# A transformer block with full attention on one core: row-maxima tables cleared on VectorE, difference tile kept longer, all loaded blocks as candidates, unit-end tasks later

## The chip, the cores and the metric

The kernel runs on one core of a Trainium2 chip. The metric is the device time of one execution in microseconds (us); three runs of the kernel before took 1124.92, 1126.49 and 1126.60 us, median 1126.49 us. Lower is better.

## What is computed

```
mod = silu(c) @ w_mod                                 # six rows of 448: sa, ca, ga, sb, cb, gb
h = layernorm(x) * (1 + ca) + sa                      # x: 2048 tokens x 448
q, k, v = h @ wqkv                                    # 16 heads of 28
p = softmax(q @ k^T * 28**-0.5)                       # 2048 x 2048 per head, no mask
x = x + ga * ((p @ v) @ wo)
h = layernorm(x) * (1 + cb) + sb
x = x + gb * (gelu(layernorm(h) @ w1 + b1) @ w2 + b2) # 448 -> 1792 -> 448
```

## The kernel before, in words

**Phase 1** normalises x, transposes it and makes q, k and v. Each matrix is kept as a high part in a short float format and a low part with the rest, so a product takes three matmul terms. q and k of the four groups of heads (g = 0 to 3, four heads each, one per 32 rows of the TensorE array) go to DRAM by blocks of 512 tokens.

**Phase 2** is the attention: 256 steps. A unit u is a group g = u // 4 and a query block qt = u % 4 of 512 queries; a step is one of the 16 key tiles (kt) of 128 keys of a unit. A step issues on TensorE twelve score matmuls (L1287): three terms for the two heads of one half of the array's rows (rows 0 to 63), and three for the other half (rows 64 to 127). ScalarE takes the exponential of each half (L1300), and TensorE multiplies by v one step later (L1245). This needs the maximum of each row of scores ahead of the unit. It is put into the score product itself, as an extra row of the q tile; so for the *next* units the scores are also computed the other way round, queries on the PSUM partitions (L474, "maximum matmuls": 128 queries by 512 keys, one head), and VectorE reduces each (L479) into a table `mxp` of the pair (g, qt). There are 1024 such matmuls. In phase 2 they stand between the score matmuls. Up to step 118 there are four in an even step and three in an odd one, on three PSUM banks (`m1`, `m2`, `m2`). From step 119 (`RING`) VectorE reduces two at a time out of a 1024-wide tile (L674), about three in a step. TensorE runs a maximum matmul of one half of the rows beside score matmuls of the other half, so `emit_single(half, ...)` looks for a head of the half that is asked for.

The order of the maximum matmuls comes from a queue `mxq`. `ready_max` keeps of its *first 64 entries* those whose q and k blocks are loaded, and `emit_single` and `emit_pair` choose from these. `count` notes what is done: when a k block has served all its maxima, the block of the next group is loaded in its place (`load_hi`, L506, one DMA on the SyncE queue); when a pair (g, qt) is complete, `max_fin` reduces its table, `put` (later) transposes the result and writes it into the q tile, and the next group's q block is loaded. A block may be used three steps after its load was issued.

Up to step 118 some blocks are done in pairs: `make_kd` forms the difference of two k blocks on GpSimd (L599); `open_pair` multiplies q with it and ScalarE takes the relu; one step later `close_pair` adds the first block's scores and takes the maximum (L638). A pair saves VectorE one reduction.

A unit's end is a chain of small tasks placed at fixed steps behind the unit's end: `t_den` (a DMA spreads the denominators), `t_rec` (VectorE reciprocal, then on SyncE a DMA to DRAM, `drec`, and a DMA that broadcasts it back to 128 rows, L998), `t_split` (GpSimd multiplies, L1003), `t_split2` (VectorE casts the high part, L1013, GpSimd makes the low part, L1014; then the DMAs out, where the unit is staged), and for the last units `t_wo`: the output projection, twelve matmuls in each of the steps kt = 8 to 11 (nine for unit 11). `load_q` loads the next unit's q tile (L760, two DMAs), and `put`'s four DMAs (L526) go into that same tile, so they wait for it.

**Phase 3** is the MLP. Its order depends on nothing that the change touches.

Every engine works through its own list in order. SyncE's list issues the DMAs, and one that waits keeps all later ones back.

Of the kernel before, what the change touches and what calls it, by code (L numbers as in the profile page):

```python
# [33 lines left out]
LAST_MAX = NKT - 4  # L34
RING = 119
PAIR_AT = (2, 2, 0, 2)
WO_MAX = 3
YTAGS = [f"{a}{i}" for a in ("kh", "qh") for i in range(4)]
EPS = 1e-5
# [4 lines left out]
def tile_adaln_block(ctx: ExitStack, tc: tile.TileContext, x, wqkv, wo, w1, b1, w2, b2, c, w_mod, out):  # L44
# [415 lines left out]
    mxp = {}  # L460
# [7 lines left out]
    def max_mm(g, qt, i, j, k, ps=None):  # L468
        if (g, qt) not in mxp:
            mxp[(g, qt)] = sbt("mxp", [128, 4, 4, 4], bufs=6)  # L470
            pool.memset(mxp[(g, qt)], -3.0e38)
        m = (ps or ps_mx)()
        js = slice(32 * j, 32 * j + DH)
        pe.matmul(m, qh_sb[(g, qt)][js, i * 128 : (i + 1) * 128], k[js, :], start=True, stop=True)  # L474
        return m
# [61 lines left out]
    phase1 = [True]  # L537
    queued = set()

    def queue_max(g, qt, cch):  # L540
        if (g, qt, cch) in queued:
            return
        queued.add((g, qt, cch))
        left.setdefault((g, qt), 64)
        if (g, qt) in paired and cch < 2:
            if cch == 1:
                pxq.extend((g, qt, i, j) for i in range(4) for j in range(4))
            return
        for i in range(4):
            for j in range(4):  # L550
                mxq.append((g, qt, cch, i, j))
        mxq.sort(key=lambda m: (m[:2] != (0, 0), -m[0] if phase1[0] else m[0], m[1:]))

    pair_no = {}

# [29 lines left out]
    def there(kind, g, b):  # L585
        return (g, b) in (qh_sb, kh_sb)[kind] and loaded.get((kind, g, b), 0) <= clock[0]

    def ready_max():
        return [m for m in mxq[:64] if there(1, m[0], m[2]) and there(0, *m[:2])][: 24 if clock[0] >= RING else 64]

    def by_set(m):
        return (m[:4], m[4] // 2)
# [1 line left out]
    kd = {"g": None, "from": 0}  # L594

    def make_kd(g):
        c0 = PAIR_AT[g]
        kd.update(g=g, t=slot("d0h", [128, 1, 512]), **{"from": clock[0] + 1})
        pool.tensor_tensor(out=kd["t"][:, 0, :], in0=f(kh_sb[(g, c0 + 1)]), in1=f(kh_sb[(g, c0)]), op=ALU.subtract)  # L599

    def other(m):
        return m[:2] + (m[2] + 1,) + m[3:]

    def pairable():
        return [
            m for m in mxq
            if m[2] == PAIR_AT[m[0]] and m[4] > 1 and other(m) in mxq and not (m[:2] == (0, 3) and m[3] > 1)
        ]

    def kept_back():  # L610
        kept = set()
        n = 0
        for m in pairable() if clock[0] < RING else ():
            n += 1
            if n <= (NKT * (m[0] * NB + m[1] - 1) + LAST_MAX - clock[0]) // 2 - 1:
                kept.update((m, other(m)))
        return kept
# [361 lines left out]
    def unit_end_tasks(u, o_sb):  # L979
# [57 lines left out]
            return go  # L1037


        times = (0, 4, 8, 9) if staged else (0, 1, 4, 5)  # L1040
        tasks = list(zip(times, (t_den, t_rec, t_split, t_split2)))
        if not staged:
            tasks += [(7 + t, t_wo(t)) for t in range(4)]
# [177 lines left out]
    def is_wo(s_):  # L1221
        return s_ // NKT >= NU - NB and 8 <= s_ % NKT < 12
# [30 lines left out]
    for u in range(NU):  # L1253
        g, qt = divmod(u, NB)
        for kt in range(NKT):
            step = u * NKT + kt
            if kt == 4 and u + 1 < NU and u + 1 not in qst:
                load_q(u + 1)
            clock[0] = step
            if kt == LAST_MAX and u + 1 < NU:  # L1260
# [3 lines left out]
                three = True  # L1264
                s_ring[:] = ["s0", turns[step % 2], turns[1 - step % 2]]
            now[0] = turns[step % 2]
            first = step % 2 if step >= RING else 0
            pt = {hf: slot(tags[step % len(tags)], [128, 2, 512], F32) for hf, tags in zip((first, 1 - first), ptags)}
            was, ring = ring, step >= RING and (three or not is_wo(step))
            if ring != was:  # L1270
                third_tile(ring)
            more = ring and not three and extra(step)
# [5 lines left out]
            ks, qs = kst[(g, kt // 4)], qst[u]  # L1278
            kc = slice((kt % 4) * 128, (kt % 4 + 1) * 128)
            for n, hf in enumerate((first, 1 - first)):  # L1280
                s2 = ps_s2() if three else ps_two((now[0] if n else "s0") if ring else ("s0", "s1")[n])
                for term, (kp, qp) in enumerate(((0, 0), (1, 0), (0, 1))):
                    if ring and n == 1 and term == 2 and mxq:
                        emit_pair(first, ps_two(turns[1 - step % 2]))
                    for jj in range(2):
                        rows_ = slice(64 * hf + 32 * jj, 64 * hf + 32 * jj + DH + (term == 0))
                        pe.matmul(s2[:, jj, :], ks[rows_, kp, kc], qs[rows_, qp, :], start=(term == 0), stop=(term == 2))  # L1287
                    if closing:
                        if (n, term) == (0, 0):
                            close_pair()  # L1290
                    elif n == 0 and term < n0 <= n_max:
                        emit_single(1, ps_mx)
                    if n == 1 and term == 2:
                        for _ in range(2 if closing else n_max - n0):
                            emit_single(0, ps_mx)
                    if ring and (n, term) == ((1, 0) if late_one else (0, 0)) and not three:
                        emit_single(1 - first, ps_mx)
                    if n == 1 and term == 2 and more:
                        emit_single(first, ps_mx)
                act.activation(pt[hf], s2, AF.Exp, scale=SCALE)  # L1300
# [131 lines left out]
```

## Time and profile before

| | |
|---|---|
| runs | 1124.92, 1126.49, 1126.60 us; median 1126.49 |
| the profiled execution's own time | 1128.93 us, span 1127.2 us |
| TensorE (PE) busy | 1113.3 us, 99% |
| VectorE (DVE) busy | 803.6 us, 71% |
| ScalarE (ACT) busy | 695.2 us, 62% |
| GpSimd (POOL) busy | 216.5 us, 19% |

One profiled execution is read. The page gives busy time by engine and groups of instructions; a group's last part is the idle time of the engine just before its instructions, with what ended it. The timeline gives single instructions as start, duration, engine, line, operation, tiles. PEld is TensorE's weight load, which overlaps the matmuls, and SPq is SyncE's queue. Step n's start is the start of its first score matmul (L1287). By these, phase 1 lasts up to 173 us, steps 0 to 118 to 480 us, steps 119 to 255 to about 831 us, the MLP to the end.

### The profile page before, as it was taken

Reading aid. Unit: us, or ns where it says so; the run is one execution under the profiler, and the core shown is the slowest. Engines: PE = TensorE matmul, PEld = TensorE weight load, DVE = VectorE, ACT = ScalarE, POOL = GpSimd, SP = SyncE. Lnnn points to the kernel's source line nnn. Section 1 sums busy time; section 2 is a strip of 40 time slices with the busy share of each in tenths; the row PEclk is TensorE's granted clock in tenths of the full one; section 3 lists DMA queues with packets and bytes.
Section 4 is the critical chain, followed back from the end, with each engine's and each line's share of the span. In section 5 each row is a group of like instructions: output and inputs, shape, how many; then the busy total and the mean of one; then the engine's idle time right before and its main releaser. Section 6 shows DMA issues by size and latency. Waiting matters only on the chain.

```text
span 1127.2 us, 20699 instructions
## 1 busy us (share of the span) xinstructions
PE 1113.3 (99%) x8319; PEld 675.3 (60%) x8319; DVE 803.6 (71%) x1380; ACT 695.2 (62%) x878; POOL 216.5 (19%) x228
## 2 busy tenths in 40 slices
PE   9999999999999999999999999999999999999998
PEld 6656765444445544444444444545468888888887
DVE  6869787979998889988888867584648853444322
ACT  4555757878888888888888867586852321111110
POOL 1543432110000000000100011205314504123000
PEclk9999999999999999999999999999999999999999
DMA  8553354131122111232210512121222100000000
GB/s 304 192 173 109 106 176 128 29 95 30 48 87 75 48 58 30 67 105 67 68 39 28 153 30 61 45 67 58 81 73 78 36 33 1 1 33 1 33 1 33
DMA packets 49342, 81.20 MB, mean 72 GB/s; under 512 B 12311, under 2 KB 18702, under 8 KB 49234
## 3 DMA queue, kind: packets, MB, share of 16 engines
q1 hardware_dynamic: 48762, 79.14, 22.5%
q8 instruction: 65, 1.06, 0.4%
q10 hardware_dynamic: 148, 0.46, 0.1%
q0 software_dynamic: 336, 0.28, 0.1%
q14 instruction: 31, 0.25, 0.1%
HBM read 55.04 MB, written 26.48 MB: 72 GB/s over the span
## 4 chain that ended last, share of the span: by engine, by line
PE 86%; DVE 2%; ACT 1%; DMA 1%; issue 1%; POOL 0%; SPq 0%; DVEq 0%; POOLq 0%; ACTq 0%
PE s L1287 21%; PE o L1245 21%; PE m L395 16%; PE m L474 7%; PE pa L395 5%; PE s L1367 3%; PE s L1368 3%; PE s L1366 3%; PE s L474 1%; PE t L1367 1%; PE t L1368 1%; PE t L1366 1%; DVE mxp L479 1%; DMA osb<-drec 1%; PE m L276 1%
## 5 line engine op out<-in xcount | busy, mean ns | idle before, releaser
L479 DVE TENSOR_REDUCE mxp<-m 128x1 f32<-128x512 f32 x564 | 364.2, 685 | 97.7 <-PE m L474 68.0
L1287 PE MATMUL s<-slot_b,slot_a 28*128 28x512 f32 (+1 forms) x3072 | 355.3, 424 | 1.7 <-DVE mxp L674 0.8
L1287 PEld LDWEIGHTS s<-slot_b,slot_a 28*128 28x128 f32 (+1 forms) x3072 | 211.1, 183 | 172.0 <-ACT slot_c L1300 93.3
L474 PE MATMUL m<-kh,qh 28*128 28x512 f32 x598 | 221.0, 462 | 2.3 <-DVE mxp L479 0.6
L1300 ACT ACTIVATE slot_c<-s 128x1024 f32<-128x1024 f32 x170 | 174.6, 1027 | 55.7 <-PE s L1287 52.4
L1245 PE MATMUL o<-slot_c,v 128*32 128x512 f32 x680 | 179.7, 607 | 0.0
L1343 ACT ACTIVATE full<-m,b_col 128x512 f32<-128x512 f32 x56 | 38.5, 688 | 191.9 <-PE m L395 179.7
L1245 PE MATMUL o<-slot_c1h,v 128*32 128x512 f32 x512 | 135.5, 608 | 0.9 <-ACT slot_c1h L1300 0.9
L1245 PE MATMUL o<-slot_c0h,v 128*32 128x512 f32 x512 | 134.7, 605 | 0.0
L1300 ACT ACTIVATE slot_c0h<-s 128x1024 f32<-128x1024 f32 x128 | 131.3, 1026 | 3.3 <-PE m L395 2.4
L674 DVE TENSOR_REDUCE mxp<-s 128x2 f32<-128x1024 f32 x105 | 128.6, 1225 | 4.2 <-PE s L474 0.2
L1300 ACT ACTIVATE slot_c1h<-s 128x1024 f32<-128x1024 f32 x128 | 130.7, 1021 | 0.0
L1346 DVE CAST hi<-full 128x512 fp32r<-128x512 f32 x56 | 25.2, 450 | 135.1 <-ACT full L1343 135.1
L1300 ACT ACTIVATE slot_d<-s 128x1024 f32<-128x1024 f32 x86 | 88.3, 1027 | 30.0 <-PE s L1287 28.4
L474 PEld LDWEIGHTS m<-kh,qh 28*128 28x128 f32 x598 | 92.4, 182 | 20.0 <-DVE mxp L479 12.0
L1003 POOL TENSOR_TENSOR osb<-osb,osb 128x512 f32<-128x512 f32 x16 | 21.1, 1318 | 398.0 <-DMA osb<-drec 332.1
L1245 PE MATMUL o<-slot_d,v 128*32 128x512 f32 x344 | 90.5, 605 | 0.4 <-ACT osb L1209 0.4
L395 PE MATMUL m<-y,slot_a 128*128 128x512 f32 x160 | 60.7, 395 | 0.0
L638 DVE CUSTOM_DVE_ANT_0 slot_d0i<-m,slot_d0i 128x512 f32<-128x512 f32 x55 | 38.0, 690 | 15.7 <-PE m L474 11.4
L1347 DVE TENSOR_TENSOR lo<-full,hi 128x512 fp32r<-128x512 f32 x56 | 44.1, 788 | 5.2
L1245 PEld LDWEIGHTS o<-slot_c,v 128*32 128x32 f32 x680 | 24.5, 108 | 38.1 <-issue 36.3
L474 PE MATMUL s<-kh,qh 28*128 28x512 f32 x210 | 46.5, 438 | 0.0
(340 smaller groups left out, 1847.4 us busy)
## 6 DMA issues: line engine op xcount, KB each, us to landing
slot_b<-d SPq DMA_DIRECT2D x32, 256.0 KB
slot_a<-d SPq DMA_DIRECT2D x32, 256.0 KB
d<-lo SPq DMA_DIRECT2D x28, 256.0 KB
d<-hi SPq DMA_DIRECT2D x16, 256.0 KB
osb<-drec SPq DMA_DIRECT2D x15, 256.0 KB
out_dram<-xn SPq DMA_DIRECT2D x16, 224.0 KB
raw<-in_B_w_dram SPq DMA_DIRECT2D x14, 224.0 KB
qh<-d SPq DMA_DIRECT2D x12, 256.0 KB
```

What stands on the lines that cost most here:

```text
L395: pe.matmul(p, a, b, start=(i == 0), stop=(i == len(terms) - 1))
L474: pe.matmul(m, qh_sb[(g, qt)][js, i * 128 : (i + 1) * 128], k[js, :], start=True, stop=True)
L479: dve.tensor_reduce(out=mxp[(g, qt)][:, i, j, cch : cch + 1], in_=m, op=ALU.max, axis=AX.X)
L674: dve.tensor_reduce(out=mxp[(g, qt)][:, i, j : j + 2, cch], in_=t, op=ALU.max, axis=AX.X)
L1245: pe.matmul(o[32 * j : 32 * j + 32, :], v_sb[kt // 4][:, kt % 4, 4 * g + j, :], p[j // 2][:, j % 2, :], start=(kt == 0), stop=(kt == NKT - 1),
L1287: pe.matmul(s2[:, jj, :], ks[rows_, kp, kc], qs[rows_, qp, :], start=(term == 0), stop=(term == 2))
L1300: act.activation(pt[hf], s2, AF.Exp, scale=SCALE)
L1343: act.activation(gf, p, AF.Gelu_apprx_tanh, bias=b1_col[:, i : i + 1])
L1347: dve.tensor_tensor(out=glo, in0=gf, in1=f(ghi), op=ALU.subtract)
L1366: pe.matmul(pp, ghi[:, ts], w_hi, start=(m == 0), stop=False)
L1367: pe.matmul(pp, ghi[:, ts], w_lo, start=False, stop=False)
L1368: pe.matmul(pp, glo[:, ts], w_hi, start=False, stop=(m == NFT - 1))
```

## The change

Nine edits, in the order of the file. (1) The tables of maxima: the table of (0, 0), all of whose entries are written anyway, is not cleared any more; those of the three pairs of phase 1 that skip an entry stay on GpSimd; the other twelve are cleared on VectorE. (2) `in_order` is the sort of `mxq` as a function; the order that it gives is the old one in phase 1, and in phase 2, where nothing of (0, 0) is left, too. (3) `ready_max` looks at all of `mxq`. (4) `make_kd` of the next group waits, two steps at a time, until no pairable block of the present one is left. (5) Which heads' rows are paired is read from `PAIR_ROWS`; the number of pairs in the program stays 55. (6) `kept_back` looks at no more pairs than there are steps for. (7) Unit-end tasks: for staged units the reciprocal and its two DMAs one step earlier, both splits one step later; for the others both splits one step later. (8) `load_q` at kt = 6 in place of 4. (9) Steps with projections take the halves in fixed order (`first` is 0 when `ring` is off), and before `RING` the two score tiles `s0` and `s1` change places.

```
-            pool.memset(mxp[(g, qt)], -3.0e38)
+            if (g, qt) != (0, 0):
+                (pool if (g, qt) in paired else dve).memset(mxp[(g, qt)], -3.0e38)
...
+    def in_order(m):
+        if phase1[0]:
+            return m[:2] != (0, 0), -m[0], m[1:]
+        return m[0], m[1], m[2:]
...
-        return [m for m in mxq[:64] if there(1, m[0], m[2]) and there(0, *m[:2])][: 24 if clock[0] >= RING else 64]
+        return [m for m in mxq if there(1, m[0], m[2]) and there(0, *m[:2])][: 24 if clock[0] >= RING else 64]
...
     def make_kd(g):
+        if g and any(m[0] == kd["g"] for m in pairable()):
+            at(clock[0] + 2, lambda: make_kd(g))
+            return
...
+PAIR_ROWS = {(0, 2): 2, (0, 3): 3, (1, 0): 2, (1, 1): 2}
-            if m[2] == PAIR_AT[m[0]] and m[4] > 1 and other(m) in mxq and not (m[:2] == (0, 3) and m[3] > 1)
+            if m[2] == PAIR_AT[m[0]] and m[4] > 1 and other(m) in mxq and m[3] < PAIR_ROWS.get(m[:2], 4)
...
-        for m in pairable() if clock[0] < RING else ():
+        for m in pairable()[: (RING - clock[0]) // 2] if clock[0] < RING else ():
...
-        times = (0, 4, 8, 9) if staged else (0, 1, 4, 5)
+        times = (0, 3, 9, 10) if staged else (0, 1, 5, 6)
...
-            if kt == 4 and u + 1 < NU and u + 1 not in qst:
+            if kt == 6 and u + 1 < NU and u + 1 not in qst:
                 load_q(u + 1)
...
-            first = step % 2 if step >= RING else 0
+            was, ring = ring, step >= RING and (three or not is_wo(step))
+            first = step % 2 if ring else 0
...
-                s2 = ps_s2() if three else ps_two((now[0] if n else "s0") if ring else ("s0", "s1")[n])
+                s2 = ps_s2() if three else ps_two((now[0] if n else "s0") if ring else ("s1", "s0")[n if step < RING else 1 - n])
```

**TensorE, steps 28 and 29.** `s` are score tiles, `m` the tiles of maximum matmuls, `o` the products with v. Before:

```order
L1287 MATMUL s_762_3134<-slot_b_426_1768,slot_a_480_1984 128x512 x6
L1287 MATMUL s_763_3142<-slot_b_426_1768,slot_a_480_1984 128x512 x6
L1245 MATMUL o_2714<-slot_d_749_3092,v_231 32x512 x2
L1245 MATMUL o_2714<-slot_c1h_3093,v_231 32x512 x2
L1287 MATMUL s_767_3158<-slot_b_426_1768,slot_a_480_1984 128x512 x6
L1287 MATMUL s_768_3166<-slot_b_426_1768,slot_a_480_1984 128x512 x6
```

After:

```order
L476 MATMUL m_762_3133<-kh_662_2745,qh_658_2725 128x512
L1297 MATMUL s_761_3130<-slot_b_426_1767,slot_a_480_1983 128x512 x2
L476 MATMUL m_763_3138<-kh_662_2745,qh_658_2725 128x512
L1297 MATMUL s_764_3144<-slot_b_426_1767,slot_a_480_1983 128x512 x6
L476 MATMUL m_765_3151<-kh_662_2745,qh_658_2725 128x512
L476 MATMUL m_766_3154<-kh_662_2745,qh_658_2725 128x512
L1255 MATMUL o_2713<-slot_d_748_3087,v_231 32x512 x2
L476 MATMUL m_771_3169<-kh_293_1249,qh_402_1680 128x512
L1297 MATMUL s_770_3166<-slot_b_426_1767,slot_a_480_1983 128x512 x4
L1297 MATMUL s_776_3186<-slot_b_426_1767,slot_a_480_1983 128x512 x6
L476 MATMUL m_777_3193<-kh_662_2745,qh_658_2725 128x512
L476 MATMUL m_778_3196<-kh_662_2745,qh_658_2725 128x512
```

The two steps had no maximum matmuls before and hold seven after (rows that only repeat are left out). At the other end, the last three projection steps with maxima (233 to 235) held eight before and hold one after.

**SyncE's queue around step 150.** `kh` and `qh` are blocks for the maxima, `slot_b` is the next unit's q tile, `drec` and `osb` the unit end's DMAs, `full` is what `put` writes. Before:

```order
L506 DMA kh_1757_7171<-d_244 128x512
L988 DMA den_7299<-osb_7267 128x1x16
L506 DMA kh_1797_7352<-d_244 128x512
L760 DMA slot_b_1798_7361<-d_235 128x512
L760 DMA slot_b_1798_7361<-d_239 128x512
L526 DMA slot_b_1798_7361<-full_7364 4x4x32 x4
L996 DMA drec_7429<-den_7299 128x16
L998 DMA osb_7431<-drec_7429 128x1x512
L506 DMA kh_1818_7441<-d_244 128x512
L506 DMA qh_1820_7446<-d_236 128x512
```

After:

```order
L998 DMA den_7319<-osb_7287 128x1x16
L508 DMA kh_1804_7372<-d_244 128x512
L1006 DMA drec_7413<-den_7319 128x16
L1008 DMA osb_7415<-drec_7413 128x1x512
L770 DMA slot_b_1820_7446<-d_235 128x512
L770 DMA slot_b_1820_7446<-d_239 128x512
L528 DMA slot_b_1820_7446<-full_7449 4x4x32 x4
L508 DMA kh_1826_7463<-d_244 128x512
L508 DMA kh_1847_7566<-d_244 128x512
L508 DMA qh_1849_7571<-d_236 128x512
```

The broadcast (`osb<-drec`) now goes ahead of the q tile and of `put`, and the k block `kh_1826` stands behind all of them. The kernel issues it in step 150, and its first maximum matmul stands in step 154, right behind that step's first two score matmuls. Before, the corresponding block `kh_1818` was issued in step 150 and first used in step 159.

**GpSimd and VectorE at the unit ends.** Before, on GpSimd, around the end of unit 9 (steps 169 to 171):

```order
L1003 TENSOR_TENSOR osb_7932<-osb_7770,osb_7932 128x512
L1014 TENSOR_TENSOR lo_8081<-osb_7932,hi_8080 128x512
L471 MEMSET mxp_8091 128x64
L515 MEMSET m_1963_8110 128x16
L1003 TENSOR_TENSOR osb_8430<-osb_8265,osb_8430 128x512
```

After, on GpSimd, the same place:

```order
L1013 TENSOR_TENSOR osb_7916<-osb_7792,osb_7916 128x512
L1024 TENSOR_TENSOR lo_8132<-osb_7916,hi_8131 128x512
L517 MEMSET m_1994_8246 128x16
L1013 TENSOR_TENSOR osb_8412<-osb_8285,osb_8412 128x512
L1024 TENSOR_TENSOR lo_8636<-osb_8412,hi_8635 128x512
```

The clearing of the tables is gone from GpSimd's list behind the splits. On VectorE the cast of the high part of unit 11 stood before in front of step 199's reductions:

```order
L674 TENSOR_REDUCE mxp_8763<-s_2149_8961 128x2
L1013 CAST hi_8972<-osb_8844 128x512
L479 TENSOR_REDUCE mxp_8763<-m_2155_8981 128x1
L674 TENSOR_REDUCE mxp_8763<-s_2157_8994 128x2
L479 TENSOR_REDUCE mxp_8763<-m_2161_9014 128x1
```

and stands behind them after, ahead of those of step 200:

```order
L684 TENSOR_REDUCE mxp_8547<-s_2156_8980 128x2
L481 TENSOR_REDUCE mxp_8547<-m_2160_8997 128x1
L684 TENSOR_REDUCE mxp_8547<-s_2162_9010 128x2
L1023 CAST hi_9021<-osb_8861 128x512
L481 TENSOR_REDUCE mxp_8547<-m_2168_9034 128x1
```

It has moved one step back.

More of the change, by code (lines that the diff above doesn't have):

```diff
@@ L551, in queue_max @@
                 mxq.append((g, qt, cch, i, j))
-        mxq.sort(key=lambda m: (m[:2] != (0, 0), -m[0] if phase1[0] else m[0], m[1:]))
+        mxq.sort(key=in_order)
     pair_no = {}
@@ L1266, in tile_adaln_block @@
             now[0] = turns[step % 2]
-            first = step % 2 if step >= RING else 0
+            was, ring = ring, step >= RING and (three or not is_wo(step))
+            first = step % 2 if ring else 0
             pt = {hf: slot(tags[step % len(tags)], [128, 2, 512], F32) for hf, tags in zip((first, 1 - first), ptags)}
-            was, ring = ring, step >= RING and (three or not is_wo(step))
             if ring != was:
```

## The prediction

> **What bounds the kernel now.** I read the page's busy times first, then the score matmuls in windows cut at step starts, then the timeline at steps that are longer than their neighbours.
>
> ```profile
> PE 1113.3 (99%) x8319; PEld 675.3 (60%) x8319; DVE 803.6 (71%) x1380; ACT 695.2 (62%) x878; POOL 216.5 (19%) x228
> ```
>
> TensorE is never long without work; no other engine is near it. The change leaves its matmuls as they are in number and shape (1024 for maxima, 3072 for scores, 1024 for v, the same projections), so it can only win or lose by how they lie beside each other and by waits. Windows of the score matmuls (the stretch, its length, busy time of matmuls and of weight loads with their number x, twelve a step with one at the edge, clock, DMA):
>
> ```profile
> 180.50:225.48 44.98, 27.13 (x217) 15.99 (x217) 1.00 0.15 40
> 225.48:417.46 191.98, 109.98 (x889) 66.52 (x889) 1.00 0.21 65
> 417.46:480.08 62.62, 37.84 (x302) 22.07 (x302) 1.00 0.14 44
> 482.59:599.22 116.63, 68.37 (x625) 41.41 (x626) 1.00 0.23 69
> 764.09:778.65 14.56, 3.60 (x36) 2.16 (x36) 1.00 0.01 1
> 805.09:823.28 18.19, 3.93 (x48) 2.09 (x48) 1.00 0.32 92
> ```
>
> Steps 2 to 19 take 44.98 / 18 = 2.50 us each, steps 94 to 118 take 62.62 / 25 = 2.50, but the 74 steps between them, 20 to 93, with fewer maxima in them, take 191.98 / 74 = 2.59. From step 120 to 171 a step takes 116.63 / 52 = 2.24. That is the first thing to see: the same work goes at two paces. Three single places lose more, and are shown with their terms. The sum is made against the profiled execution, 1128.93 us (span 1127.2); the median of the runs, 1126.49, lies 2.4 lower, and I take that difference off at the end.
>
> **The change, part by part.**
>
> *Candidates from the whole queue, with the pair rules and the difference tile kept (edits 2 to 6).* In the built order before, steps 20 to 93 hold two steps with no maxima (28, 29) and some 28 steps with maxima beside score matmuls of their own half of the array, where the two cannot run together, since the first 64 entries of the queue offered no other; the order after has the pattern of steps 2 to 19 throughout, but for four steps (72 to 78, even) with two such maxima. VectorE's share in the pattern is the same as in steps 2 to 19, where it fits. Pairs stay 55. So 74 x 2.50 = 185.0. The 7.0 us that the stretch takes above that, over the 28 steps, are 0.25 a step; four such steps remain, 1.0. That gives 186.0 against 191.98, -6.0. Bounds: 0, if something other than the order made those steps slow, and -7.0.
>
> The maxima so moved forward are missing at the end: steps 232 to 235 are projection steps, the last three going from eight maxima to one. Three such steps with maxima take 14.56 / 3 = 4.85, four without 18.19 / 4 = 4.55, so about -0.8. But in steps 229 to 231 the order after has only maxima of the wrong half left; at the same 0.25 a step, +0.8. Together 0 (-0.8 to +1).
>
> *Tables not cleared on GpSimd (edit 1).* In phase 1:
>
> ```profile
> 30.35 0.50 PE L474 MATMUL ma<-kh,qh 28*128 28x512 f32 x2
> 33.55 0.50 PE L474 MATMUL m<-kh,qh 28*128 28x512 f32 x1
> 33.72 0.16 POOL L471 MEMSET mxp<- 128x64 f32 x1
> 33.91 1.29 DVE L479 TENSOR_REDUCE mxp<-ma 128x1 f32<-128x512 f32 x2 [3.76 <-POOL mxp L471]
> 34.66 1.09 PE L474 MATMUL ma<-kh,qh 28*128 28x512 f32 x2 [0.61 <-DVE mxp L479]
> 36.28 0.50 PE L395 MATMUL pa<-slot_b,slot_a 128*128 128x512 f32 x1
> ```
>
> VectorE had the first maxima before it since 30.85 and waited for a clearing that GpSimd reached at 33.72. The next four maxima then took 36.28 - 33.55 = 2.73 us for lack of banks; with banks free, heads of four row groups go side by side in about 0.5. Without the clearing, VectorE has all four first tiles done by 33.7: up to -2.2, at least the 0.61 of marked idle time. I take -1.9; VectorE, busy behind it, moves earlier as well. In phase 2 (unit 9's end):
>
> ```profile
> 597.67 1.28 POOL L1014 TENSOR_TENSOR lo<-osb,hi 128x512 fp32r<-128x512 f32 x1 [3.44 <-DVE hi L1013]
> 598.89 0.15 POOL L471 MEMSET mxp<- 128x64 f32 x1
> 599.08 0.69 DVE L479 TENSOR_REDUCE mxp<-m 128x1 f32<-128x512 f32 x1 [1.48 <-POOL m L515]
> 599.22 0.50 PE L1287 MATMUL s<-slot_b,slot_a 29*128 29x512 f32 x2
> 602.85 0.50 PE L1287 MATMUL s<-slot_b,slot_a 29*128 29x512 f32 x2
> ```
>
> Here a clearing stood behind the low part; VectorE waited 1.48, and the step took 3.63 in place of 2.24. On VectorE the clearing stands in front of the reduction that needs it: -1.3. The twelve clearings there, at GpSimd's 0.15 to 0.3 each, lie in steps where VectorE has that much room; uncovered they would cost 1.8 to 3.6 in all.
>
> *Splits one step later (edit 7).* At the first projection step, 200:
>
> ```profile
> 662.15 1.28 POOL L1003 TENSOR_TENSOR osb<-osb,osb 128x512 f32<-128x512 f32 x1 [25.80 <-DMA osb<-drec]
> 663.41 0.50 PE L1287 MATMUL s<-slot_b,slot_a 29*128 29x512 f32 x2
> 663.46 0.43 DVE L1013 CAST hi<-osb 128x512 fp32r<-128x512 f32 x1 [2.02 <-POOL osb L1003]
> 664.54 0.49 PE L474 MATMUL m<-kh,qh 28*128 28x512 f32 x1 [0.62 <-DVE mxp L479]
> 666.71 1.07 PE L1245 MATMUL o<-slot_c1h,v 128*32 128x512 f32 x2
> 671.14 0.73 PE L1287 MATMUL s<-slot_b,slot_a 29*128 29x512 f32 x5
> 675.31 0.49 PE L1287 MATMUL s<-slot_b,slot_a 29*128 29x512 f32 x2
> 711.09 0.49 PE L1287 MATMUL s<-slot_b,slot_a 29*128 29x512 f32 x2
> 716.67 0.72 PE L1287 MATMUL s<-slot_b,slot_a 29*128 29x512 f32 x5
> ```
>
> VectorE stood 2.02 us at the cast, with step 199's reductions behind it, and TensorE ran out of banks. Step 200 took 7.73 us. The cast now comes behind those reductions, at about 663.7, when GpSimd is done (663.43). The first projection step of the next unit took 5.58; with nine projection matmuls for twelve (step 201 takes 4.17, against 4.85) that makes 4.9: -2.8 (-1.0, the marked waits alone, to -3.5). The low part moves from 665.2 to 665.5, still ahead of the first projection matmul. For unit 14 the later cast costs: it now falls behind the reductions of weights that end at 808.2, so the low part is ready at 808.2 + 0.43 + 1.29 = 809.9, where its matmul stood at 809.35: +0.5 (0 to 1).
>
> ```profile
> 805.91 1.29 POOL L1014 TENSOR_TENSOR lo<-osb,hi 128x512 fp32r<-128x512 f32 x1 [2.69 <-DVE hi L1013]
> 807.52 0.69 DVE L1133 TENSOR_TENSOR slot_a<-raw,slot_b 128x512 fp32r<-128x512 f32 x1
> 809.35 0.36 PE L395 MATMUL m<-slot_e,lo 128*128 128x448 f32 x1
> ```
>
> *SyncE's queue (edits 7 and 8, with 3).* The reciprocal's DMAs now go ahead of the q tile and of `put`; around step 150 a k block stands behind them all, first used in step 154.
>
> ```profile
> 248.69 0.86 SPq L506 DMA_DIRECT2D kh<-d  x2
> 252.53 0.46 PE L474 MATMUL m<-kh,qh 28*128 28x512 f32 x1 [0.57 <-DMA kh<-d]
> 548.53 2.61 SPq L526 DMA_DIRECT2D slot_b<-full  x4
> 551.24 0.43 SPq L996 DMA_DIRECT2D drec<-den  x1
> 552.76 0.55 SPq L998 DMA_DIRECT2D osb<-drec  x1
> 558.62 1.28 POOL L1003 TENSOR_TENSOR osb<-osb,osb 128x512 f32<-128x512 f32 x1 [31.36 <-ACT slot_d L1300]
> ```
>
> From the start of step 149: reciprocal and `drec` issue 0.6, broadcast issued 551.24 to 552.76 = 1.5 later, landed by 558.62 = 5.9 after that; the q tile, behind it in the queue, lands with it; `put`'s four issues 2.7; then the k block, 252.53 - 248.69 = 3.8. Sum 14.5 us. Step 154 starts 5 x 2.24 = 11.2 us after step 149. TensorE waits +3.3 (0 to +5) with everything queued behind that matmul. Taking the Trainium skill's fit in "DMA: Bandwidth & Descriptors", section "Anatomy of one DMA — SWDGE (gpsimd) path" (2.0 us and bytes over 436 GB/s), a 256 KB transfer would land in an estimated 2.6 us and the sum would be 10.0, with no wait; both rows above are longer, and I go by the rows. The other blocks used three steps after their loads (steps 32, 86, 142, 150, 156) stand behind no broadcast: 3.8 against at least 5 us, no wait, at a cost of 3 each if that fails.
>
> *Score tiles (edit 9).*
>
> ```profile
> 170.33 0.59 ACT L487 ACTIVATE slot_d0h<-ma 128x512 f32<-128x512 f32 x1
> 172.50 0.53 ACT L457 COPY v<-pa 128x448 f32<-128x448 f32 x1 [0.66 <-PE pa L395]
> 173.08 0.50 PE L1287 MATMUL s<-slot_b,slot_a 29*128 29x512 f32 x2 [0.62 <-ACT v L457]
> ```
>
> `s0` takes the banks of `pa`, `s1` those of `ma`. Step 0 waited 0.62 for `pa`; it now begins in the banks of `ma`, free at 170.9: -0.6 (0 at least). At step 119 it is the other way: `s0` was written last in step 118; I put +0.2 on the exponential (0 to 0.5). The halves' fixed order in projection steps I cost at nothing: steps 201 and 202 begin with different halves and the windows show one pace.
>
> Sum: -6.0 + 0 - 1.9 - 1.3 - 2.8 + 0.5 + 3.3 - 0.6 + 0.2 = -8.6, so 1120.3 for a profiled execution and, with the 2.4 off, 1117.9 as a median.
>
> **The rivals.** *No wait at step 154:* the broadcast or the k block lands sooner; -11.9, 1114.6. For it: the stop of 0.57 above is the only one by a load that I found in this phase. Against: the 5.9 us. The Trainium skill's fit is on this side. *The wait slows the clock:* soon after the wait of 0.62 at 664.54 a product with v took 1.07, and the granted clock of that stretch fell to 0.91 of full:
>
> ```profile
> 660.00:680.00 20.00, 18.98 (x141) 9.99 (x139) 9.25 (x14) 11.30 (x13) 4.84 (x4) 0.91 0.05 13
> ```
>
> 0.09 x 20 = 1.8 us are lost; the same after step 154 gives -6.8, 1119.7. The Trainium skill ("TensorE: Matmul & The Clock Gate", section "Part 1: The HAM clock gate (the "warmup" mystery)") has the clock halved after an idle window of about 3.4 us; a wait of 3.3 is nearly that, though the trace shows the fall after less. *VectorE sets the pace of steps 20 to 93:* the row of the page has it at 71% over all, far more in these steps, so rearranging gives nothing; -2.6, 1123.9. Against: steps 94 to 118 hold more maxima and are faster. *Slower:* the blocks at three steps' distance all land late, since loads now start in the same steps as the units' own; five waits of 3.3 more, and one slowed clock each (1.8): -8.6 + 25.5, so 1143.4; it decides for slower from 2.2 us a wait. *It changes nothing that counts:* the sort is the old one, but the order shows the moves, so only cancellation is left; 1126.
>
> **How the numbers follow.** Forecast 0.53, no wait 0.18, slowed clock 0.16, VectorE's pace 0.07, slower 0.04, nothing 0.02. The likeliest is 1117.9. The range, 1112.0 to 1122.5, takes in the first three with the bounds of their terms and leaves out the last three (0.13). A difference under 0.2% (2.3 us) is about what a measurement cannot tell from none. Faster 0.91 (the first three and, at 2.6 us, 0.04 of VectorE's case), same 0.05 (the rest of that case and nothing), slower 0.04.
>
> **What would show it.** Right: steps 20 to 93 in about 186 us; no wait of VectorE for GpSimd at 33 and around step 172; step 200 near 5 us; TensorE waiting for a `kh` DMA in step 154 by some 3 us. Wrong: a pace of 2.59 kept in steps 20 to 93, waits for `kh` at steps 32, 86 or 142, or VectorE waiting in front of its clearings.

## The result and the profile after

| | before | after |
|---|---|---|
| median of 15 runs, us | 1126.49 (1124.92 to 1127.48) | 1122.42 (1118.96 to 1125.30) |
| ratio, 95% interval | | 0.9963 (0.9954 to 0.9973) |
| profiled execution, us (span) | 1128.93 (1127.2) | 1122.83 (1120.9) |

Forecast were 1117.9 us and a gain of 8.6; the gain is 4.07. The two profiled executions lie 6.1 apart. What stands out is the spread: the runs after reach over 6.3 us, those before over 2.6.

The engines' busy times on the page of the changed kernel:

```profile
PE 1105.9 (99%) x8319; PEld 669.6 (60%) x8319; DVE 807.3 (72%) x1393; ACT 693.9 (62%) x878; POOL 214.9 (19%) x215
```

TensorE still bounds it. Windows of all engines, cut at the step starts of the changed kernel (stretch, its length, busy time of PE, PEld, DVE, ACT and POOL with their numbers x, granted clock, DMA share, GB/s). The rows are steps 20 to 93, 94 to 118, 154, 172, 200, 229 to 231, 232 to 235, and 248:

```profile
220.80:406.79 185.99, 185.99 (x1779) 88.39 (x1776) 169.58 (x319) 159.91 (x187) 16.85 (x19) 1.00 0.22 66
406.79:469.87 63.08, 62.88 (x604) 29.62 (x600) 57.50 (x108) 55.04 (x65) 2.62 (x3) 1.00 0.14 40
548.44:555.30 6.86, 3.60 (x27) 1.15 (x23) 2.37 (x4) 2.73 (x3) 0.00 (x0) 0.84 0.38 116
593.86:596.12 2.26, 2.26 (x27) 0.98 (x23) 2.25 (x4) 1.94 (x3) 1.34 (x2) 1.00 0.31 116
656.61:661.58 4.97, 4.86 (x36) 2.75 (x32) 2.65 (x5) 2.73 (x3) 1.29 (x1) 1.00 0.02 4
742.29:752.38 10.09, 9.31 (x73) 4.04 (x69) 5.89 (x8) 5.89 (x7) 1.26 (x1) 0.83 0.25 69
752.38:771.86 19.48, 19.34 (x136) 12.05 (x133) 7.77 (x20) 10.21 (x12) 8.04 (x8) 1.00 0.04 8
798.28:803.39 5.11, 4.81 (x33) 2.85 (x33) 4.44 (x7) 2.88 (x4) 1.33 (x1) 1.00 0.50 143
```

Steps 20 to 93 take 185.99 us, 6.0 less than before. Step 172 fell from 3.63 to 2.26, step 200 from 7.7 to 4.97. Against that, step 154 takes 6.86 in place of 2.28, and steps 229 to 231 take 10.09 in place of 6.7; in both rows the clock is down, which it is in no other.

Phase 1, timeline of the changed kernel around the first maxima:

```profile
28.90 0.50 PE L476 MATMUL ma<-kh,qh 28*128 28x512 f32 x2
29.44 1.29 DVE L481 TENSOR_REDUCE mxp<-ma 128x1 f32<-128x512 f32 x2 [0.74 <-PE m L476]
30.64 1.28 DVE L481 TENSOR_REDUCE mxp<-m 128x1 f32<-128x512 f32 x2
32.09 0.49 PE L476 MATMUL m<-kh,qh 28*128 28x512 f32 x1
32.09 0.49 PE L476 MATMUL ma<-kh,qh 28*128 28x512 f32 x2
32.10 0.50 PE L476 MATMUL m<-kh,qh 28*128 28x512 f32 x1
```

VectorE starts 0.54 after the first maximum matmul, where it waited 3.76 for GpSimd's clearing before, and the next maxima, at 32.09, find free banks and run side by side. From the first projection matmul to step 0 it is now 168.18 - 23.67 = 144.51 us, before 173.08 - 25.13 = 147.95. The first projection matmul itself came 1.46 earlier; in the other profiles, of whichever kernel, it lies anywhere between 23.4 and 25.3, so that is the execution's, not the change's.

The chain that ended last, in order of time, in the stretch before step 154's stop (start, length, what):

```profile
539.83 5.86 DMA slot_b<-d
...
545.74 0.55 SPq L528
...
548.07 3.99 DMA kh<-d
552.06 0.14 issue
552.20 0.46 PE m L476
```

This is the queue as the prediction had it: the q tile, in flight together with the broadcast, lands 5.86 after its issue, then `put`, then the k block with 3.99, and TensorE, which began step 154 at 548.44, stands until 552.20.

The same windows view, cut now at the edges of the slowed clock:

```profile
549.66:553.08 3.42, 0.88 (x13) 0.76 (x13) 0.38 (x1) 0.11 (x1) 0.00 (x0) 1.00 0.69 207
553.08:556.49 3.41, 3.41 (x25) 1.25 (x23) 1.76 (x3) 1.83 (x2) 0.00 (x0) 0.50 0.00 0
...
744.23:747.64 3.41, 2.63 (x27) 1.28 (x23) 2.45 (x4) 2.28 (x4) 1.26 (x1) 1.00 0.22 65
747.64:751.05 3.41, 3.41 (x22) 1.54 (x15) 0.97 (x2) 1.01 (x1) 0.00 (x0) 0.50 0.00 0
```

Twice the clock is at half for 3.41 us: once behind the stop at step 154, once behind one in step 230. If half the work is done in 3.41 us at half clock, each costs 3.41 / 2 = 1.7, an estimate; the first experiment has steps 229 to 231 without the slowed stretch, 8.52 us for 10.09, which is 1.57. (The clock falls a third time at 1119.7 us, behind the last matmul, where it costs nothing.) The second stop, on TensorE and VectorE:

```profile
745.22 0.69 DVE L481 TENSOR_REDUCE mxp<-m 128x1 f32<-128x512 f32 x1 [0.23 <-PE m L476]
746.06 0.69 DVE L481 TENSOR_REDUCE mxp<-s 128x1 f32<-128x512 f32 x1
746.80 0.49 PE L476 MATMUL s<-kh,qh 28*128 28x512 f32 x1 [0.78 <-DVE mxp L481]
747.33 0.69 DVE L481 TENSOR_REDUCE mxp<-s 128x1 f32<-128x512 f32 x1 [0.58 <-PE s L476]
748.18 1.07 PE L1255 MATMUL o<-slot_c1h,v 128*32 128x512 f32 x2
```

This is the place where only maxima of the wrong half of the array are left: no pair of heads fits the wide tile, two single maxima take its place, and the second waits for VectorE to finish the first.

### The profile page after: what moved, and what is told of

Its sections match the earlier page's. It is cut to its first block, busy times and chain, and to the rows that moved or that the text cites. A ratio compares the mean times of both kernels' runs of the same rounds, so it can differ in the third digit from the quotient of the medians.

```text
span 1120.9 us, 20683 instructions
## 1 busy us (share of the span) xinstructions
PE 1105.9 (99%) x8319; PEld 669.6 (60%) x8319; DVE 807.3 (72%) x1393; ACT 693.9 (62%) x878; POOL 214.9 (19%) x215
## 4 chain that ended last, share of the span: by engine, by line
PE 92%; DVE 3%; DMA 2%; ACT 1%; issue 1%; SPq 0%; POOL 0%; DVEq 0%; ACTq 0%; POOLq 0%
PE s L1297 22%; PE o L1255 22%; PE m L396 16%; PE pa L396 8%; PE m L476 8%; PE s L1377 3%; PE s L1378 3%; PE s L1376 3%; DVE mxp L481 2%; PE s L476 2%; PE t L1377 1%; PE t L1378 1%; PE t L1376 1%; PE ma L476 1%; DMA slot_c<-in_w_mod_dram 1%
## 5 line engine op out<-in xcount | busy, mean ns | idle before, releaser
L1297 PE MATMUL s<-slot_b,slot_a 28*128 28x512 f32 (+1 forms) x3072 | 360.0, 425 | 0.5 <-ACT slot_c0h L1310 0.5
L476 PEld LDWEIGHTS m<-kh,qh 28*128 28x128 f32 x598 | 89.8, 182 | 20.6 <-DVE mxp L481 12.3
```

## The experiments

Each was timed beside fresh runs of the kernel before; ratios are to those. Where a kernel is compared with the changed one, it is by the two ratios (0.0010 is 1.1 us). "Undone" means taken out of the changed kernel.

**SyncE's order put back.**

```
-        times = (0, 3, 9, 10) if staged else (0, 1, 5, 6)
+        times = (0, 4, 9, 10) if staged else (0, 1, 5, 6)
...
-            if kt == 6 and u + 1 < NU and u + 1 not in qst:
+            if kt == 4 and u + 1 < NU and u + 1 not in qst:
```

> From the changed kernel, only the order on SyncE's queue is put back: load_q at kt = 4, and the staged units' reciprocal with its two DMAs one step later, so the k block that step 154 uses stands behind the broadcast alone and no longer behind the q tile and put as well. Theory W (the stop at step 154 and the slowed clock behind it are lost to that queue): step 154 goes from 6.86 to about 2.3 us, step 155 from 2.66 to 2.3, the profiled span from 1120.9 to about 1116, the median to 1117 to 1118.5. Rival 1 (the block lands no sooner, since the broadcast alone holds it back): step 154 keeps a stop of over 1 us and the median stays above 1120. Rival 2 (the loss at step 154 was mainly the clock of that one execution): the stop goes, but the median moves by less than 2.5 us.

Measured: median 1118.20, ratio 0.9921 (0.9908 to 0.9933), 4.7 us faster than the changed kernel. Steps 154, 200 and 229 to 231:

```profile
549.19:552.07 2.88, 2.59 (x27) 1.10 (x23) 2.15 (x4) 2.13 (x3) 1.27 (x1) 1.00 0.59 184
652.86:657.82 4.96, 4.85 (x36) 2.74 (x33) 2.64 (x5) 2.72 (x3) 1.29 (x1) 1.00 0.02 4
738.50:747.02 8.52, 7.74 (x73) 3.41 (x69) 5.89 (x8) 5.90 (x7) 1.27 (x1) 1.00 0.28 80
```

Theory W holds: of the 4.6 us by which step 154 had grown, 0.6 are left, and the clock stays full. Step 230's stop is still there, at full clock: 8.52 where 6.7 stood before, so the stop costs 1.8 by itself, and the rest of its 3.4 is the clock.

**Splits put back.**

```
-        times = (0, 3, 9, 10) if staged else (0, 1, 5, 6)
+        times = (0, 3, 8, 9) if staged else (0, 1, 4, 5)
```

> From the changed kernel, both splits of a unit's end one step earlier again (staged and not staged); nothing else moves on TensorE. Theory A of the prediction (step 200 loses 2.8 us by the cast in front of the reductions): step 200 back to 7.7, step 248 back to 4.55, the median 2.2 us above the changed kernel. Theory B (of these 2.8 only 1.0 to 1.1 is the two marked waits; the other 1.7 us was one stretch of 3.4 us at half clock, which not every execution has): step 200 takes 6.0 where the clock stays full and 7.7 where it falls, and the median moves by +0.5 to +1.5 us.

Measured: median 1122.47, ratio 0.9954 (0.9938 to 0.9970). Steps 200, 229 to 231, and 248:

```profile
656.43:661.41 4.98, 4.88 (x36) 2.75 (x33) 2.44 (x4) 2.73 (x3) 0.00 (x1) 1.00 0.02 4
742.13:753.02 10.89, 10.11 (x73) 4.08 (x69) 7.09 (x10) 6.72 (x7) 2.56 (x2) 0.76 0.25 67
799.05:803.60 4.55, 4.55 (x33) 2.85 (x32) 4.29 (x8) 2.82 (x4) 1.29 (x1) 1.00 0.47 118
```

Both theories fall at step 200: it stays at 4.98 with the cast in front of the reductions again. Step 248 falls by 0.56, as forecast, and the median does not rise, though both theories said that it would. Behind the stop in step 230 the clock stays at half for two such stretches in a row here, 747.79 to 754.62 us, so one stop can cost more than one of them.

**First 64 entries again.**

```
-        return [m for m in mxq if there(1, m[0], m[2]) and there(0, *m[:2])][: 24 if clock[0] >= RING else 64]
+        return [m for m in mxq[:64] if there(1, m[0], m[2]) and there(0, *m[:2])][: 24 if clock[0] >= RING else 64]
```

> From the changed kernel, only the look at the whole queue is taken back (first 64 entries again); the difference tile, the pairs' rows and kept_back stay new. In the built order ten steps between 20 and 93 then break the pattern (26 to 29, 33, five even ones from 74 to 82), against five in the changed kernel and over thirty before; steps 229 to 231 have maxima of both halves again; and the k blocks of the last group are used in steps 152, 156 and 161, not in 154. Theory (each broken step costs what it cost before): steps 20 to 93 take 187.5 to 188.5 us (186.0 in the changed kernel, 192.0 before), step 230 falls from 4.56 to 2.3 and 231 from 3.18 to 2.2, the stop moves from step 154 to 152 and is smaller (2 us); in all 1 to 4 us faster than the changed kernel. Rival (looking at the whole queue is what the gain of steps 20 to 93 comes from): 190 us or more there.

Measured: median 1119.03, ratio 0.9929 (0.9917 to 0.9941). Steps 20 to 93, 229 to 231, and 232 to 235, then from the timeline the stop in step 150:

```profile
221.88:408.65 186.77, 186.76 (x1772) 88.89 (x1768) 165.00 (x311) 160.28 (x187) 16.79 (x19) 1.00 0.22 65
740.54:747.25 6.71, 6.71 (x73) 2.87 (x69) 5.74 (x7) 5.82 (x7) 1.29 (x1) 1.00 0.37 103
747.25:768.14 20.89, 20.79 (x143) 13.24 (x140) 11.81 (x26) 10.14 (x12) 7.81 (x8) 1.00 0.00 1
```

```profile
543.35 0.50 PE L476 MATMUL s<-kh,qh 28*128 28x512 f32 x1 [0.78 <-DVE mxp L481]
```

The look at the whole queue brings 0.8 in steps 20 to 93, less than expected, and costs more later: without it the kernel is 3.8 us faster. Steps 229 to 231 are as before. Step 154 takes 2.16: no matmul waits for a k block there or, as was expected, in step 152. In its place step 150 has a stop like the one in step 230, a second single maximum that waits for VectorE (steps 150 to 152 take 8.14 for 6.70). Steps 232 to 235 take 1.4 more. All five runs have a clock of 1.000, with this one stop left in them.

**Difference tile and pairs as before.**

```
-        if g and any(m[0] == kd["g"] for m in pairable()):
-            at(clock[0] + 2, lambda: make_kd(g))
-            return
...
-            if m[2] == PAIR_AT[m[0]] and m[4] > 1 and other(m) in mxq and m[3] < PAIR_ROWS.get(m[:2], 4)
+            if m[2] == PAIR_AT[m[0]] and m[4] > 1 and other(m) in mxq and not (m[:2] == (0, 3) and m[3] > 1)
...
-        for m in pairable()[: (RING - clock[0]) // 2] if clock[0] < RING else ():
+        for m in pairable() if clock[0] < RING else ():
```

> From the changed kernel, edits 4 to 6 (difference tile kept until its pairs are issued, rows of pairs by table, kept_back cut to the steps left) are taken back; the look at the whole queue stays. The built order then breaks the pattern in 33 steps between 20 and 96, as many as before. Theory (the gain of steps 20 to 93 comes from the difference tile and the pairs, not from the longer look): those steps take 190.5 to 192.5 us, and the median is 4 to 6 us above the changed kernel, slower than the kernel before. Rival (the longer look carries the gain): 187 us or less there, and the median within 2 us of the changed kernel.

Measured: median 1129.16, ratio 1.0018 (1.0009 to 1.0027). Steps 20 to 93, and 229 to 231:

```profile
220.87:411.89 191.02, 190.67 (x1777) 92.97 (x1774) 169.74 (x319) 161.77 (x187) 16.75 (x18) 1.00 0.21 61
748.44:756.89 8.45, 7.67 (x73) 3.33 (x69) 5.90 (x8) 5.89 (x7) 1.27 (x1) 1.00 0.30 84
```

So 5.0 of the 6.0 gained in steps 20 to 93 come from the difference tile and the pairs. Without them the rest of the change is slower than the kernel before. Step 154 takes 6.61 with the clock at half behind it, as in the changed kernel, but the stop in step 230 leaves the clock full.

**The kernel before, once more.** Unchanged, one profile.

> The kernel before, unchanged, profiled once more. Theory C (the 2.75 us that step 200 lost were an accident of the one profiled execution: the small DMA to drec landed after 2.67 us where it takes 1.4 to 1.5 in the other profiles, the broadcast and the cast came that much later, and half a window of slowed clock followed): step 200 takes 4.9 to 6.0 us here and the execution lies at 1125 to 1127. Rival (the cast in front of the reductions always costs it): step 200 takes 7.7 again.

Measured: 1127.59 us. Its windows row of step 200, then, from the DMA view of 653 to 656 us, the queues (packets, MB, share):

```profile
664.07:669.65 5.58, 5.22 (x37) 2.81 (x34) 3.40 (x5) 2.83 (x3) 1.23 (x1) 1.00 0.02 4
```

```profile
q1 hardware_dynamic: 144, 0.01, 3.4%
q8 instruction: 1, 0.02, 2.7%
```

Step 200 takes 5.58, not 7.7: 1.7 of the first profile was a stretch at half clock, which this one has at another place (35.6 us). But the small DMA to `drec` is late here too (2.6 us). It is no accident of one execution: in both, 16 KB of program text are fetched by DMA in just these microseconds (queue `instruction`, one packet). Theory C is half right.

**All of edits 7 and 8 undone.**

```
-        times = (0, 3, 9, 10) if staged else (0, 1, 5, 6)
+        times = (0, 4, 8, 9) if staged else (0, 1, 4, 5)
...
-            if kt == 6 and u + 1 < NU and u + 1 not in qst:
+            if kt == 4 and u + 1 < NU and u + 1 not in qst:
```

> From the changed kernel, the whole of edits 7 and 8 taken back: both splits one step earlier, the staged units' reciprocal one step later, load_q at kt = 4; the maxima stay new. Theory C (step 200 does not depend on these two edits but on when one DMA lands): step 200 takes 4.9 to 6.0, step 248 4.55, the stop at step 154 shrinks to 0.6 as with the queue alone put back, and the median is 4 to 5.5 us below the changed kernel, 1117 to 1118. Rival 1 (either edit alone is enough to spare step 200, and without both it loses 2.75): step 200 at 7.7 and a median of 1120 to 1121. Rival 2 (the moves of the unit ends are worth their 2.3 net as forecast): above 1121.

Measured: median 1116.78, ratio 0.9916 (0.9905 to 0.9928). Step 200, and the DMA view of 641.5 to 644.6 us, in which `drec` is written:

```profile
652.33:657.30 4.97, 4.86 (x36) 2.75 (x33) 2.52 (x4) 2.73 (x3) 0.07 (x1) 1.00 0.02 4
```

```profile
q1 hardware_dynamic: 147, 0.01, 4.0%
```

No program text passes, the DMA lands after 1.45, and step 200 takes 4.97 with neither edit. Theory C holds: moving the unit ends brought step 200 nothing; a program with other instructions fetches its text at other moments. The thirteen profiles agree on the DMA to `drec` of unit 11: in five of them (the two of the kernel before, the two experiments that start from it, and the one with the first 64 entries) a fetch of 16 KB begins 0.2 to 0.3 us behind its issue, and it lands after 2.2 to 2.7; in the other eight none begins in that time, and it lands after 1.4 to 1.5. Edits 7 and 8 together cost 5.3 us by the ratios.

**Clearing on GpSimd again.**

```
-            if (g, qt) != (0, 0):
-                (pool if (g, qt) in paired else dve).memset(mxp[(g, qt)], -3.0e38)
+            pool.memset(mxp[(g, qt)], -3.0e38)
```

> From the changed kernel, all tables of maxima cleared on GpSimd again, (0, 0) too. Theory (the clearing held VectorE up at 33 us and in step 172, as the prediction has it): the first projection matmul behind the maxima of (0, 0), the 34th, comes 11.1 us after the first one as in the kernel before (8.9 in the changed kernel), step 172 takes 3.6 in place of 2.26, and the median is 3.2 to 4 us above the changed kernel. Rival (phase 1 takes the time back in a later wait, since DMAs and GpSimd bound it there): step 0 starts at most 1 us later than in the changed kernel, and the median is 1.5 to 2.5 us above it.

Measured: median 1125.94, ratio 0.9996 (0.9987 to 1.0006). Phase 1, and the window of step 172:

```profile
32.20 0.15 POOL L472 MEMSET mxp<- 128x64 f32 x1
32.39 1.29 DVE L480 TENSOR_REDUCE mxp<-ma 128x1 f32<-128x512 f32 x2 [3.77 <-POOL mxp L472]
```

```profile
596.97:599.23 2.26, 2.26 (x28) 0.97 (x25) 2.25 (x4) 1.94 (x3) 1.41 (x3) 1.00 0.30 114
```

By the ratios it is 3.7 us slower than the changed kernel, as expected. VectorE's wait of 3.77 is back, and step 0 comes 2.7 later behind the first projection matmul (147.22 for 144.51). But step 172 stays at 2.26: with the split a step later the clearing no longer stands behind the low part. With the splits alone put back (second experiment) it is short as well, 2.29. Either edit is enough for it.

**No stops: 51 pairs, queue back, short splits.**

```
-PAIR_ROWS = {(0, 2): 2, (0, 3): 3, (1, 0): 2, (1, 1): 2}
+PAIR_ROWS = {(0, 2): 2, (0, 3): 3, (1, 0): 2, (1, 1): 1}
...
-        return [m for m in mxq if there(1, m[0], m[2]) and there(0, *m[:2])][: 24 if clock[0] >= RING else 64]
+        return [m for m in mxq if there(1, m[0], m[2]) and there(0, *m[:2])][:64]
...
-        times = (0, 3, 9, 10) if staged else (0, 1, 5, 6)
+        times = (0, 4, 9, 10) if staged else (0, 1, 4, 5)
...
-            if kt == 6 and u + 1 < NU and u + 1 not in qst:
+            if kt == 4 and u + 1 < NU and u + 1 not in qst:
```

> A version without the three stops: from the changed kernel, one row fewer of pairs in (1, 1), 51 pairs in place of 55; 64 ready entries also from step 119 on; SyncE's queue as before (load_q at kt = 4, the staged reciprocal one step later); the splits of units that are not staged one step earlier. In the built order no k block is used under six steps from its load after step 119, and steps 229 to 231 have maxima of both halves. Theory (stop at 154, stop at 230 with the clock that each slows, and the late cast at 248 are what the changed kernel lost): steps 154 and 230 at 2.3, step 248 at 4.55, steps 20 to 93 at 186 to 187, no stretch of slowed clock, and a median of 1114.5 to 1116. Rival (the stops only come up elsewhere, as the tables still have to be full by the unit's start): 1118 or more.

Measured: median 1115.06, ratio 0.9892 (0.9877 to 0.9906), 8.0 us faster than the changed kernel. Steps 154 and 229 to 231:

```profile
549.82:552.10 2.28, 2.28 (x27) 1.02 (x23) 2.05 (x3) 1.92 (x3) 1.83 (x2) 1.00 0.06 22
738.88:745.60 6.72, 6.72 (x74) 2.90 (x70) 6.02 (x8) 5.83 (x7) 2.56 (x2) 1.00 0.36 104
```

Both stops are gone, nothing came in their place, and all of its runs have a granted clock of 1.000.

**Later splits alone, on the kernel before.** `times = (0, 4, 9, 10) if staged else (0, 1, 5, 6)`.

> From the kernel before, only the splits one step later (edit 7 without the reciprocal's move). Both profiles of the kernel before have the 16 KB of program text that are fetched at 653 us in the same moment as the packets to drec, which land after 2.6 us in place of 1.4; the cast then holds VectorE 1.4 to 2.0 us. Theory D (the prediction's mechanism is real but needs this late DMA): step 200 takes 4.95 in place of 5.6 (7.7 with slowed clock), step 172 falls to 2.3 since the low part now stands behind the clearing, step 248 rises to 5.1; net -1.4 us at full clock, a median of 1124.5 to 1125.5. Rival (the split is not what holds step 200): step 200 stays at 5.5 or above.

Measured: median 1125.50, ratio 0.9991 (0.9982 to 1.0000). Steps 172, 200 and 248:

```profile
597.83:600.10 2.27, 2.27 (x29) 0.98 (x25) 2.23 (x5) 1.94 (x3) 1.23 (x1) 1.00 0.24 85
660.67:665.66 4.99, 4.87 (x36) 2.75 (x32) 2.66 (x5) 2.75 (x3) 1.29 (x1) 1.00 0.02 4
799.66:804.77 5.11, 4.81 (x34) 2.85 (x33) 4.38 (x7) 2.88 (x4) 1.33 (x1) 1.00 0.49 141
```

Where `drec` is late (2.23 us here), the later cast does what the prediction said of it: 4.99 for 5.58. The mechanism was right; in the changed kernel nothing was left for it.

**Score tiles exchanged back, on the version with 51 pairs.**

```
-("s1", "s0")[n if step < RING else 1 - n]
+("s0", "s1")[n]
```

> From the version with 51 pairs and no stops, the score tiles s0 and s1 change places again before step 119, as in the kernel before. Theory (step 0 waits 0.6 for the banks of the last copy of v): step 0 starts 0.6 later behind the first projection matmul, 145.3 in place of 144.7 us; steps 94 to 118 go back from 63.0 to 62.65 us and step 119 from 2.13 to 2.5; in all +0.3 to +0.6 us, 1115.3 to 1115.8. Rival (the places of the tiles matter to nothing): within 0.2 us, step 0 at 144.7.

Measured: median 1114.95, ratio 0.9896 (0.9883 to 0.9910). Steps 94 to 118:

```profile
408.29:471.00 62.71, 62.71 (x606) 29.55 (x602) 57.45 (x108) 54.79 (x65) 2.61 (x3) 1.00 0.15 48
```

Step 0 comes 0.63 later behind the first projection matmul (145.32 for 144.69), steps 94 to 118 take 0.3 less, step 119 0.24 more. The parts came out as expected; their sum is too small for these runs, and the median, expected 0.3 us or more higher than with 51 pairs, is not.

**Clearing moved alone, on the kernel before.** The diff of edit 1.

> From the kernel before, only edit 1: (0, 0) not cleared, twelve tables cleared on VectorE. Theory: phase 1 gains 2.6 to 2.8 us (as the changed kernel lost by the reverse), step 172 falls from 3.63 to 2.3, steps 20 to 93 keep their 192, step 200 keeps its late cast unless the fetch of program text falls elsewhere (5.0 to 5.6 at full clock); and the stop at 33 us, which can slow the clock, is gone. Median 1121.5 to 1122.5, as much as the whole change brought. Rival (VectorE pays for the clearings where it has most to do, steps 2 to 118, 0.2 each): steps 2 to 118 0.5 or more slower.

Measured: median 1122.25, ratio 0.9958 (0.9945 to 0.9972). Phase 1 and steps 20 to 93:

```profile
30.02 1.29 DVE L480 TENSOR_REDUCE mxp<-ma 128x1 f32<-128x512 f32 x2 [0.75 <-PE m L475]
```

```profile
222.08:413.44 191.36, 191.28 (x1770) 93.46 (x1766) 165.54 (x312) 161.77 (x187) 16.75 (x18) 1.00 0.21 65
```

The first of nine edits alone brings what all nine bring. Phase 1 gains 2.6 (145.35 for 147.95), step 172 takes 2.31, and its five runs have a clock of 0.999 or 1.000. Step 200 takes 5.66, a little over what was expected: the cast is early and `drec` late, as before.

## Why the prediction was wrong, point by point

| term | forecast | the two profiles | at full clock, by the experiments |
|---|---|---|---|
| steps 20 to 93 | -6.0 | -5.99 | -6.0 |
| phase 1's clearing, step 0 | -2.5 | -3.44 | -3.4 (2.7 and 0.6 by undoing) |
| step 172 | -1.3 | -1.37 | -1.4 |
| step 200 | -2.8 | -2.75 | -0.6, and not by the splits |
| step 248 | +0.5 | +0.56 | +0.6 |
| steps 154, 155 | +3.3 | +5.09 | +3.4 |
| steps 229 to 231 | +0.8 | +3.37 | +1.8 |
| steps 232 to 235 | -0.8 | -0.68 | -0.7 |
| all other steps | +0.2 | +0.40 | +0.4 |
| sum | -8.6 | -4.81 | -5.9 |

The two spans differ by 6.3: the 4.8, and the 1.46 by which the first projection matmul came earlier. Of the 8.6 us forecast, 4.07 came. As is worked out below, about 2.0 of the 4.5 that are missing are missing at full clock already, and 2.5 went to slowed clocks.

Right were the clearing of (0, 0) (0.9 too small), the q tile's queue in front of step 154 with its price (3.3 forecast, 3.4 without the clock), step 248, and step 0's wait for the score tiles. None of the five other blocks at three steps' distance was late. The rival of no wait did not come: the q tile landed 5.86 us after its issue, the k block 3.99.

Right in number, but not in its reason, was the pace of steps 20 to 93. The prediction blamed the first 64 entries of the queue, which "offered no other" head. With these 64 put back the steps still take 186.77; it is the difference tile and the pairs that carry 5.0 of the 6.0. The loss by the score tiles was put on step 119 (+0.2), which got 0.37 shorter (2.51 to 2.14); it came in steps 94 to 118 (62.62 to 63.08). In the rival of five late blocks the border of 2.2 us a wait leaves out the 1.8 that it counts for each slowed clock; with them the border is 0.4.

Three steps failed. *Step 200* was sized at -2.8 from one execution in which 1.7 was half clock; and its cause, a DMA of 8 KB that took 2.67 us where one without a fetch beside it takes 1.4 to 1.5, stands in none of its rows. Program text was fetched at that moment; in the changed kernel it is fetched at another. The *2.4 us taken off for the median* took it that the profiled execution of the changed kernel would lie as far above its median; it lies 0.4 above. Part of the stretch at half clock may have been counted twice by this, but that is not shown: of 49 runs of the kernel before, timed beside the experiments, 32 have a granted clock of 0.998 or less, as the profiled one has, so most of them seem to have lost such a stretch too. The profiled one also has its first projection matmul at 25.13 us, late among the profiles.

*Steps 229 to 231* were priced "at the same 0.25 a step" as the steps before 119. There the maxima have three banks of their own; here two singles share one wide tile and the second waits for VectorE, which costs 1.8 (8.52 for 6.72 at full clock).

*The clock* was a rival at 0.16 and is what happened, at two places where one was thought of. The runs tell how often. Granted clock and time of the changed kernel's 15 runs lie on one line:

| granted clock | runs | us |
|---|---|---|
| 1.000 | 2 | 1118.96, 1119.42 |
| 0.998 | 4 | 1121.21 to 1122.11 |
| 0.996, 0.997 | 5 | 1122.02 to 1122.83 |
| 0.995 | 2 | 1123.10, 1123.99 |
| 0.993 | 2 | 1125.15, 1125.30 |

Its median lies 3.2 above its two runs at full clock (1119.2). A clock of 0.999 can be the stretch behind the last matmul alone, as in the profile with the tiles exchanged back (from 1111.70 us on, the only one). The kernel before has a median of 1125.75 over its runs at 0.999 or 1.000 (17 of 49, of three sessions), and 1126.5 to 1126.9 over all: it loses 0.8 to 1.1. At full clock the change would so be worth 6.6 (5.9 by the terms; 0.7 is not assigned); some 2.5 of it go to slowed clocks, 4.1 stay. That the stops bring them is shown by their removal: with the first stop cut to 0.6 to 0.8 us, eight of nine runs have 0.999 or 1.000 and one 0.996; with one stop of VectorE's left alone (first 64 entries) all five have 1.000, and with both gone all four. Only one execution of each kernel shows where its clock fell. A run at 0.993 must have lost more than two such stretches, since the profiled one with two has 0.996; where is not known.

The Trainium skill ("TensorE: Matmul & The Clock Gate", section "Part 1: The HAM clock gate (the "warmup" mystery)") has the clock judged in free-running windows of 3413 ns. The trace agrees: the two slowed stretches begin 747.64 - 553.08 = 194.56 us apart, 57.0 times 3.413, and each lasts 3.41. It also says that an idle window halves the clock. Here the window ahead of the second stretch held 2.63 us of matmuls out of 3.41, so less than an idle window was enough; the measurement decides. The matmul time in a window does not decide alone either. The same stop of 0.78 left the clock full with SyncE's order put back, with edits 7 and 8 undone, and with the pairs as before, where the first stop had slowed the clock and the window of the second (749.84 to 753.25) held 2.62. The rule for how little work is too little stays open.

## What to carry to other kernels

A place that takes long in one profile has to be found in a second one before its price goes into a sum, above all when that profile lies above the median: what made it slow may not belong to the kernel, and taken off again at the end it can count twice. A stop of the bounding engine is priced with the clock it can cost, and a load that is moved in a queue with all that stands in front of it. When a change of many edits moves the time little, try the edits one by one: here one of nine brought all of the 4 us, the pairs 5 more, two others cost 5 and a third 3.8. Each is measured with the others in place, so they do not add up.

## What the runs showed of the hardware

The program's own text is fetched by DMA while the kernel runs, here mostly 16 KB at a time (65 packets of 16 KB in each of the two first profiles). Beside one such fetch a DMA of 8 KB landed after 2.6 us in place of 1.4, at the same place in both profiles of the same program; in the changed kernel with edits 7 and 8 undone no fetch fell there, and it took 1.45.

Where the clock fell with matmuls still to come, it was at half for 3.41 us or for twice that. So the same stop of 0.78 us in step 230 cost steps 229 to 231 1.8 us in one execution, 3.4 in another (one stretch at half clock) and 4.2 in a third (two). A kernel with such stops shows it in the spread of its runs: 6.3 us with both, and with the first one reduced 1.0 us over four runs and 2.8 over five.
